# A fused attention and FFN block: seven products for eight in more of the first FFN product, with fills, row scales and loads rearranged

## The chip, the cores and the metric

The kernel runs on one core of one Trainium2 chip. The metric is the device time of one execution in microseconds (us). A kernel is run several times, and medians are quoted. The profile is that of one execution. It gives a *span*, the time from the core's first to its last recorded work. The listed time is a little longer than the span, by 1.2 to 1.6 us here, and that difference matters below.

Names used: PE is TensorE, PEld its weight load, DVE is VectorE, ACT is ScalarE, POOL is GpSimd, SP is SyncE. A *bank* is a PSUM bank of 512 fp32 columns. "K tile t" is the product that makes the keys of 128 tokens (10 PE instructions of 320 columns). A "chunk" is 512 tokens, and there are four of them.

## The reference

```python
def _layernorm(x, axis=-1, eps=1e-5):
    m = jnp.mean(x, axis=axis, keepdims=True)
    v = jnp.var(x, axis=axis, keepdims=True)
    return (x - m) / jnp.sqrt(v + eps)

# x (1, 2048, 640) bf16, wqkv (640, 1920), wo (640, 640), w1 (640, 1728), w2 (1728, 640)
def _A_ref(x, wqkv, wo):              # linear attention, 32 heads of 20
    qkv = (x @ wqkv).reshape(B, S, 3, H, Dh).transpose(2, 0, 3, 1, 4)
    q, k, v = qkv[0], qkv[1], qkv[2]
    phi = lambda t: jnp.where(t > 0, t + 1, jnp.exp(t)) + 1e-6
    pq, pk = phi(q), phi(k)
    kv = jnp.einsum("bhsd,bhse->bhde", pk, v)
    z = jnp.einsum("bhsd->bhd", pk)
    num = jnp.einsum("bhqd,bhde->bhqe", pq, kv)
    den = jnp.einsum("bhqd,bhd->bhq", pq, z)[..., None] + 1e-6
    return (num / den).transpose(0, 2, 1, 3).reshape(B, S, D) @ wo

def _B_ref(x, w1, w2):                # FFN: relu(x w1) w2
    return jnp.maximum(x @ w1, 0) @ w2

xn = _layernorm(x)
out = x + _A_ref(xn, wqkv, wo) * silu(_B_ref(xn, w1, w2))
```

## The kernel before

The first FFN product makes a transposed hidden layer `hT`: 13 blocks of 128 rows and a half block of 64, for each of the four chunks, each block five products of 512 columns along the contraction (640 = 5 x 128). Chunks 2 and 3 already go through a scheme of seven products for eight over 2 x 2 blocks: blocks i and i + 6, chunks 2 and 3, four of the five contraction tiles; the fifth is added as it is. Chunks 0 and 1 are done block by block, with the other products woven in:

```python
def H_mm(j, f, b=None):                     # a block of the first FFN product, conventionally
    b = nextb() if b is None else b
    src, keys = hsrc(j)
    sc.group("PE", [(lambda eng, k=k: eng.matmul(ps[b], lhsT=w1_col(k, P * f, P), rhs=src[:, k, :],
                                                 start=(k == 0), stop=(k == C - 1))) for k in range(C)], ...)
    return lambda: sc.op("ACT", ...activation(out=hT[:, f, schunk(j)], in_=ps[b], func=ACTF.Relu)...)
# ...
kat = [{5: 4, 7: 5, 9: 6, 11: 7}, {2: 8, 5: 9, 8: 10, 11: 11, 14: 12, 16: 13, 18: 14, 20: 15}]
lnat = [{9: 8, 11: 9}, {0: 10, 2: 11, 5: 12, 8: 13, 11: 14, 13: 15}]
for j in range(2):
    for n, item in enumerate(plans[j]):
        # ... Q_block or H_block
        if j == 1 and n == 0:
            scale_bcast()
            build_consts()                  # GpSimd's fills and masks
        if j == 1 and n >= 7 and n < 20:
            scale_h(n - 7)                  # chunk 0 of hT times its row scales, on VectorE
        # ...
        if n in kat[j]:                     # one K tile after every second or third block
            t = kat[j][n]
            K_mm(t, 0)
            K_exp(t, 0)
            K_relu(t, 0)
            K_fin(t)
```

The tokens of chunk 0 go into the first products centred but not yet divided by their deviation, so that PE can start early; the first blocks of `hT` are scaled afterwards. The scales come from a diagonal matrix that GpSimd makes and one product with ones:

```python
def scale_rows():
    sc.op("POOL", ... tensor_tensor(out=dg..., in0=ident..., in1=rsy[:, 0:4]..., op=ALU.mult) ...)
def scale_bcast():
    b = nextb()
    sc.group("PE", [lambda eng: eng.matmul(ps[b], lhsT=one, rhs=dg, start=True, stop=True)], ...)
```

A unit of the scheme (`h_unit`), its sums on VectorE and copies on ScalarE, with PE's products marked `mm`:

```python
def s1():  mm(1, ba, True); cp(ps[bb], ("ps", bb), ba)      # ScalarE writes one bank from another
def s5_(): mm(5, bc, True); cp(s5, skey, bc, ...)
def s6():  mm(6, ba);       tt(ps[bc], ps[ba], s5, ALU.add, ...)   # VectorE, in PSUM
def s2():  mm(2, bb);       relu("ACT", i, 2, bb)
def s7():  mm(7, ba);       cp(ps[bd], ("ps", bd), ba)
def s3():  mm(3, bc);       relu("ACT", i, 3, bc)
def s4():
    mm(8, ba)
    tt(dst, ps[ba], s5, ALU.add, ...)                        # VectorE, PSUM to SBUF
    # ... a max on VectorE
    mm(4, bd); relu("DVE", i + 6, 2, bd)
```

The place later in the kernel that the change touches too: `u_T(4)` is a sum of 2240 columns on VectorE that is wanted late, `kvs()` makes the masked copies of kv that the products with wo (`W_block`) want at once.

```python
divide(0)
load_recip(1)
load_recip(2)
u_T(4)
# ...
        if p == 0:
            if n == 0:
                kvs()
            if n == 1:
                W_block(0, 4)
```

## Time and profile before

| | before |
|---|---|
| time, median of 3 | 209.35 us (209.14 to 209.63) |
| profiled span | 209.0 us |
| listed time less span, all its runs in this study | 1.21 to 1.31 us |
| spans of its 34 timed runs beside the experiments | 207.6 to 209.5 us, median 208.2 |
| first 512-column product to first wo product, profiled run | 12.66 to 133.03 = 120.37 us |

The last row is *the stretch*. It starts with the first conventional FFN product, behind the head in which PE waits for data to land, and ends with the first product with wo. All of the change but its head lies inside.

How to read the views: in the chain of waits and the timeline the first two numbers are start and duration in us, then engine, tile and line. On the PE, pieces of the chain that abut are work back to back. L650 is the conventional FFN block, L1029 a product of the seven-for-eight scheme, L551 a K tile, L601 a Q block, L819 a sum or product of two tensors on VectorE, L1277 a wo product.

Three cautions. In the chain a piece that follows other work begins where that work ends, some 0.17 us after its own first instruction; a piece that follows a wait begins with its own first instruction. So 120.37 is 0.16 too short: by the first instructions in the timeline, 12.50 and 133.03 us, the stretch of before is 120.53. For the same reason the idle time in square brackets is some 0.16 us less than what the wait costs. And where a record of a product is missing (x29 for x30), the chain shows 0.05 us of "issue" that is no wait.

One thing beside the lines that the prediction shows: the timeline of GpSimd and VectorE where the masks are built.

```profile
35.34 1.80 POOL L433 MEMSET regH<- 128x2048 bf16 x1
35.43 1.94 DVE L489 TENSOR_SCALAR reg<-reg,mv,rsy 128x640 bf16<-128x640 bf16 x1 [0.99 <-POOL rsy L469]
```

This norm on VectorE ends at 37.37 us, 0.23 us after GpSimd's fill. Elsewhere a norm takes 0.39 to 0.45 us, but for one of 1.15 us at 19.33, beside GpSimd's 1.03 us for the diagonal matrix (19.27). The change moves the fill and drops the matrix.

### The profile page before, as it was taken

What the parts mean: (1) busy time and instruction counts of PE and PEld (TensorE: products, weight loads), DVE (VectorE), ACT (ScalarE), POOL (GpSimd) and SP (SyncE); (2) the same over time, 40 slices, a digit from 0 to 9 for tenths busy, and PEclk for the clock granted to TensorE, in tenths of its full rate; (3) what the DMA queues carried; (4) which work ended last, traced back from release to release, by engine and by line L of the source; (5) the groups of instructions that cost most, each with busy time, mean ns of one, the idle gap of its engine ahead of it and who ended that gap; (6) DMA issues with size and microseconds to landing.
All of it is one profiled execution on the core that took longest, in us unless ns stands there. A gap on an engine that the chain in (4) does not pass through costs nothing.

```text
span 209.0 us, 3733 instructions
## 1 busy us (share of the span) xinstructions
PE 205.1 (98%) x1401; PEld 127.0 (61%) x1401; DVE 165.0 (79%) x365; ACT 120.8 (58%) x243; POOL 21.3 (10%) x54
## 2 busy tenths in 40 slices
PE   8999999999999999999999999999999999999995
PEld 7755555545555444444456777677777777777773
DVE  3888757768999858686879759898888989897465
ACT  6497767787787987786563435362435254343531
POOL 1176015711210000000000000000000000000001
DMA  6998896130136000301224999246941010110103
GB/s 196 330 297 168 219 257 94 31 63 2 39 59 186 0 5 0 125 0 26 102 63 108 245 343 376 98 123 219 362 148 63 3 63 28 38 63 0 63 3 127
DMA packets 33063, 24.74 MB, mean 118 GB/s; under 512 B 12821, under 2 KB 33045, under 8 KB 33045
## 3 DMA queue, kind: packets, MB, share of 16 engines
q1 hardware_dynamic: 31813, 23.13, 39.2%
q10 hardware_dynamic: 1232, 1.37, 1.9%
q8 instruction: 11, 0.18, 0.4%
q14 instruction: 7, 0.06, 0.1%
HBM read 15.81 MB, written 5.24 MB: 101 GB/s over the span
## 4 chain that ended last, share of the span: by engine, by line
PE 86%; DVE 6%; DMA 5%; issue 1%; SPq 0%
PE psT L874 33%; PE psT L650 14%; PE psT L1029 11%; PE psT L551 11%; PE psT L601 10%; DMA reg<-in_B_w_dram 4%; DVE reg L819 2%; PE psT L1486 2%; DMA reg<-in_A_x_dram 1%; PE psT L668 1%; PE psT L1277 1%; DVE reg L1474 1%; DVE regE L819 1%; PE psT L525 1%; DVE pqT L812 1%
## 5 line engine op out<-in xcount | busy, mean ns | idle before, releaser
L874 PE MATMUL psT<-reg,regH 128*128 128x320 bf16 (+1 forms) x224 | 34.3, 299 | 0.0
L874 PE MATMUL psT<-reg 128*128 128x320 bf16 (+1 forms) x164 | 27.7, 299 | 0.0
L874 PEld LDWEIGHTS psT<-reg,regH 128*128 128x128 bf16 (+1 forms) x224 | 21.9, 98 | 8.5
L819 DVE TENSOR_TENSOR psT<-psT,reg 128x320 f32<-128x320 f32 (+1 forms) x33 | 16.4, 513 | 12.0 <-PE psT L874 8.8
L1311 ACT ACTIVATE wv_sb<-psT 128x320 bf16<-128x320 f32 x28 | 11.3, 436 | 25.2 <-PE psT L874 15.6
L601 PE MATMUL psT<-reg 128*128 128x512 bf16 x100 | 24.7, 379 | 0.0
L561 ACT ACTIVATE regE<-psT 128x640 bf16<-128x640 f32 x24 | 15.6, 701 | 8.1 <-PE psT L551 8.1
L874 PEld LDWEIGHTS psT<-reg 128*128 128x128 f16 (+1 forms) x164 | 16.0, 98 | 6.9 <-DVE regH L819 0.2
L881 ACT ACTIVATE psT<-psT 128x320 f32<-128x320 f32 x32 | 13.6, 426 | 11.2 <-PE psT L874 10.7
L881 ACT ACTIVATE reg<-psT 128x320 f32<-128x320 f32 (+1 forms) x24 | 10.4, 435 | 15.6 <-PE psT L874 13.6
L650 PE MATMUL psT<-reg 128*128 128x512 bf16 x75 | 18.5, 379 | 0.0
L654 ACT ACTIVATE regH<-psT 128x512 bf16<-128x512 f32 x28 | 16.5, 608 | 3.2 <-PE psT L650 3.2
L551 PE MATMUL psT<-reg 128*128 128x320 bf16 x120 | 18.3, 299 | 0.0
L461 DVE BATCH_NORM_STATS2 stats<-reg 128x6 f32<-128x320 bf16 x32 | 14.1, 475 | 4.7 <-DMA reg<-in_A_x_dram 4.7
L601 PEld LDWEIGHTS psT<-reg 128*128 128x128 bf16 x100 | 9.6, 98 | 11.0 <-issue 0.7
L551 PEld LDWEIGHTS psT<-reg 128*128 128x128 bf16 x120 | 11.7, 98 | 6.5
L1479 POOL TENSOR_TENSOR reg<-reg 128x224 bf16<-128x224 bf16 x1 | 0.6, 604 | 146.6 <-DVE reg L1474 146.6
L819 DVE TENSOR_TENSOR reg<-reg 128x1024 f16<-128x1024 bf16 (+6 forms) x17 | 13.6, 809 | 2.3 <-DMA reg<-in_B_w_dram 2.0
L650 PE MATMUL psT<-regX,reg 128*128 128x512 bf16 x65 | 14.8, 379 | 0.0
L874 PE MATMUL psT<-reg,pqT 128*128 128x320 bf16 (+1 forms) x72 | 14.7, 299 | 0.0
L1474 DVE TENSOR_TENSOR reg<-psT,wv_sb 128x640 bf16<-128x640 f32 (+2 forms) x16 | 11.7, 739 | 3.4 <-PE psT L874 1.8
L1029 PE MATMUL psT<-reg 128*128 128x512 bf16 x48 | 14.0, 379 | 0.0
(145 smaller groups left out, 354.1 us busy)
## 6 DMA issues: line engine op xcount, KB each, us to landing
reg<-in_B_w_dram SPq DMA_DIRECT2D x12, 320.0 KB, 6.0
scr<-rden SPq DMA_DIRECT2D x4, 640.0 KB, 8.8
reg<-in_A_x_dram SPq DMA_DIRECT2D x4, 640.0 KB, 6.5
out_dram<-reg SPq DMA_DIRECT2D x15, 160.0 KB, 1.9
reg<-in_A_x_dram SPq DMA_DIRECT2D x13, 160.0 KB, 5.0
regE<-scr SPq DMA_DIRECT2D x3, 640.0 KB, 8.1
reg<-in_A_wo_dram SPq DMA_DIRECT2D x6, 160.0 KB, 3.1
reg<-in_A_wqkv_dram SPq DMA_DIRECT2D x1, 800.0 KB, 5.3
```

What stands on the lines that cost most here:

```text
L461: sc.op("DVE", lambda eng: eng.bn_stats(stats[:, t, a, :], xv[:, HN * a:HN * (a + 1)]), R=[("xin", t % XR)], W=[("stats", t, a)])
L551: fns.append(lambda eng, a=a, k=k, lhs=lhs: eng.matmul(ps[b + a][:, 0:HN], lhsT=lhs, rhs=wk[:, k, HN * a:HN * (a + 1)], start=(k == 0), st ...
L561: sc.op("ACT", lambda eng: eng.activation(out=o_.rearrange("p (a n) -> p a n", a=2), in_=ps2(b, HN), func=func, scale=scale), R=[("ps", b) ...
L601: sc.group("PE", [(lambda eng, k=k: eng.matmul(ps[b], lhsT=wq[:, k, P * f:P * (f + 1)], rhs=xnT[:, j, k, :], start=(k == 0), stop=(k == C ...
L650: sc.group("PE", [(lambda eng, k=k: eng.matmul(ps[b], lhsT=w1_col(k, P * f, P), rhs=src[:, k, :], start=(k == 0), stop=(k == C - 1))) for ...
L654: return lambda: sc.op("ACT", lambda eng: eng.activation(out=hT[:, f, schunk(j)], in_=ps[b], func=ACTF.Relu), R=[("ps", b)], W=[("hT", j, f)])
L819: sc.op("DVE", lambda eng: eng.tensor_tensor(out=out, in0=in0, in1=in1, op=op), R=R, W=W, extra=extra)
L874: sc.group("PE", [(lambda eng, k=k, lhs=lhs, rhs=rhs: eng.matmul(ps[b][:, 0:HN], lhsT=lhs, rhs=rhs, start=(start and k == 0), stop=(k == n ...
L881: sc.op("ACT", lambda eng: eng.activation(out=dst, in_=ps[b][:, 0:HN], func=ACTF.Copy), R=[("ps", b)], W=[dkey], extra=extra)
L1029: sc.group("PE", [(lambda eng, k=k, lhs=lhs, rhs=rhs: eng.matmul(ps[b], lhsT=lhs, rhs=rhs, start=(start and k == 0), stop=(k == n - 1), sk ...
L1311: sc.op("ACT", lambda eng: eng.activation(out=g[:, HN * n:HN * (n + 1)], in_=ps[b][:, 0:HN], func=ACTF.Silu), R=[("ps", b)], W=[("g", sl, ...
L1474: sc.op("DVE", lambda eng: eng.tensor_tensor(out=tmpo[:, os_, lo:hi].rearrange(shp, a=na), in0=src, in1=g_of(t)[0][:, lo:hi].rearrange(shp ...
```

## The change

Intent: use the seven-for-eight scheme for chunks 0 and 1 too, in four of its six block pairs (blocks 0 to 3 with 6 to 9). Five blocks (4, 5, 10, 11, 12) stay conventional and come first, while x is still being normalised and transposed. K tiles 4 to 7 are made in a row between the two chunks of these blocks; one K tile goes into each unit. To make room on VectorE and GpSimd, the fill and the masks move to the idle head, the row scales come from four small products, and most of the scalings fall away, since the four units take normalised tokens. Weight pieces 2 and 5 are loaded first, being wanted first. `u_T(4)` moves behind the kv copies.

The diff, cut to its core:

```diff
     sc.op("DVE", lambda eng: eng.memset(zero[:, :], 0.0), W=[("zero",)])
+    sc.op("DVE", lambda eng: eng.memset(hT[:, NF, :], 0.0), W=[("hz",)])
 ...
-    w1_load(0, 2, "SP")
+    w1_load(2, 3, "SP")
+    w1_load(5, 6, "SP")
     x_load(4)
     x_load(5)
-    w1_load(2, 3, "SP")
+    w1_load(6, NW, "SP")
     x_load(6)
     x_load(7)
-    w1_load(3, NW, "SP")
+    for d in (0, 3):
+        w1_load(d, d + 1, "SP")
 ...
     def build_consts():
-        sc.op("POOL", lambda eng: eng.memset(hT[:, NF, :], 0.0), W=[("hz",)])
 ...
+    build_consts()
 ...
+        if whole:
+            fns.append(lambda eng: eng.matmul(ps[b][:, HN:512], lhsT=one, rhs=wk[:, 0, 0:512 - HN], start=False, stop=True,
+                                              skip_group_check=True))
 ...
-        sc.group("PE", [lambda eng: eng.matmul(ps[b], lhsT=one, rhs=dg, start=True, stop=True)], R=[("dg",)],
-                 W=[("ps", b)])
+        sc.group("PE", [(lambda eng, t=t: eng.matmul(
+            ps[b][:, P * t:P * (t + 1)], lhsT=rsyH[:, t:t + 1].to_broadcast([P, P]), rhs=ident[:, :],
+            start=True, stop=True)) for t in range(4)], R=[("rsyH",), ("ident",)], W=[("ps", b)])
 ...
-    kat = [{5: 4, 7: 5, 9: 6, 11: 7}, {2: 8, 5: 9, 8: 10, 11: 11, 14: 12, 16: 13, 18: 14, 20: 15}]
 ...
+    HP = (4, 5, 10, 11, 12)
 ...
+    for n, f in enumerate(HP):
+        H_block(0, f)
+        run(after[n])
+        if n == 3:
+            x_load(8, 2)
+            w_load(wq[:, :, :], A_wqkv[:, 0:D], ("wq",))
+    scale_rows()
 ...
+    for n in range(4):
+        K_tile(4 + n, 2 * (n % 2))
+        run(after[n])
+    x_load(10, 2)
 ...
+        if n == 1:
+            x_load(12, 2)
+            x_load(14, 2)
+            for d in (1, 4):
+                w1_load(d, d + 1, "SP")
 ...
+    units = [h_unit(i, 0) for i in range(4)]
 ...
+    units[0]["s1"]()
+    for i, u in enumerate(units):
+        ob = 4 * (i % 2)
+        t = 8 + i
+        u["s5"]()
+        K_mm(t, ob + 2, whole=True)
+        K_exp(t, ob + 2)
+        u["s6"]()
+        K_relu(t, ob + 2)
 ...
+    build_mv6()
 ...
-    u_T(4)
 ...
                 if n == 0:
                     kvs()
+                    u_T(4)
```

The variable `whole` adds a product over the 192 columns of a bank that the K tile leaves unwritten, because the next unit lets ScalarE write that bank and then adds products to it.

## The prediction

> **What bounds the kernel now.** I read three views in this order: the busy digits of the page (which engine has no gap), the chain of waits in order of time (is that engine's work really what the end follows back to), and the timeline where the change puts work.
>
> ```profile
> PE 205.1 (98%) x1401; PEld 127.0 (61%) x1401; DVE 165.0 (79%) x365; ACT 120.8 (58%) x243; POOL 21.3 (10%) x54
> ...
> PE   8999999999999999999999999999999999999995
> ```
>
> A full digit for PE is no proof, since ends of matmuls are modelled. The chain decides: its pieces abut, and their length is instruction count times a fixed pitch.
>
> ```profile
> 9.68 2.99 PE psT L551 x22
> 12.66 6.47 PE psT L650 x30
> 19.14 1.36 PE psT L551 x10
> 20.50 2.16 PE psT L650 x10
> 22.66 1.36 PE psT L551 x10
> ...
> 131.29 1.69 DVE reg L819 x2
> 132.98 0.05 issue
> 133.03 0.87 PE psT L1277 x4
> ```
>
> Read: 30 products of 512 columns in 6.47 us are 215.7 ns each, 10 of 320 columns in 1.36 us are 136 ns each, and each piece begins where the last ended. From 9.68 to about 114 us nothing but PE is on the chain, so there a product removed is worth its pitch, and nothing else is worth anything unless it makes PE wait. The last three lines show the one wait of PE behind another engine in the middle of the kernel. Its timeline:
>
> ```profile
> 130.07 1.60 PE L1251 MATMUL psT<-reg,wv_sb 128*128 128x120 bf16 x30
> ...
> 131.21 1.32 DVE L819 TENSOR_TENSOR reg<-reg,regX 128x2240 f16<-128x2240 bf16 x1
> ...
> 132.44 0.95 DVE L819 TENSOR_TENSOR reg<-psT,mv 128x360 bf16<-128x360 f32 x3
> ...
> 133.03 0.87 PE L1277 MATMUL psT<-reg 128*128 128x320 bf16 x4 [0.41 <-DVE reg L819]
> ```
>
> VectorE does a 2240-wide sum (u_T(4), needed only at the end of that unit) before the masked copies of kv that PE waits for; PE loses 0.41 us.
>
> **What the Trainium skill says.** (1) "TensorE: Matmul & The Clock Gate", section "Wait — 56ns, not 53.3ns?": warm back-to-back products start every N / 2.4 GHz + about 2.5 ns, 215.7 ns at N = 512. The trace agrees (215.7), and five 128-column transposes in 0.28 us agree with its 55.6. (2) "VectorE: DVE Perf Modes", section "Zero memsets can be issued as uint32 (trn2)": a memset takes a cycle per element whatever its type, and zeros may be issued as 4-byte words. At the page's 0.96 GHz I estimate 2.1 us for the 2048-wide fill, 1.1 us if issued as words; the trace has none of that size on VectorE. (3) "SBUF — State Buffer", section "Who interferes with whom": VectorE in a two-port mode and GpSimd block each other for a whole instruction. The trace agrees: the normalising step normally takes about 0.45 us and took 1.94 us at 35.43 beside GpSimd's 1.80 us fill at 35.34. (4) "PSUM — Partial Sum Buffer", section "The four PSUM rules": a first product clears the written bits of its whole bank, and ScalarE's writes don't set them. That is why the change adds a product over the other 192 columns after some K products; the trace of before has no such case.
>
> **The change part by part.**
>
> 1. Chunks 0 and 1 of the first FFN product. Before: 13 blocks x 2 chunks x 5 = 130 products of 512 columns. After: five blocks (4, 5, 10, 11, 12) as before, 5 x 2 x 5 = 50, and four units of 7 x 2 + 4 = 18 each, 72, in place of 80. Removed: 8 x 0.2157 = 1.73 us of PE. This is small because the five tiles along the contraction leave one that isn't shared out: 18 for 20, not 7 for 8. The half block is still 20 small products.
> 2. Added on PE: four 192-column products. Estimate from the skill's formula 192 / 2.4 + 2.5 = 82 ns, 0.33 us together. The row-scale broadcast goes from one 512-column product (0.22 us in the chain) to four of 128 (4 x 0.056 = 0.22 us): nothing.
> 3. u_T(4) moves after the kv products. VectorE reaches the masked copies at 131.2 instead of 132.44 us; three take 0.95 us, the first product of kv ended about 130.9, so they are done before PE has finished the seven products that start at 131.51 and end at 132.62. The 0.41 us wait should vanish.
> 4. VectorE: removed nine of 14 scalings at about 0.41 us (3.7 us). Added four 1024-wide sums of x, 4 x 0.69 = 2.7 us, and per unit one PSUM sum (0.70), one PSUM-to-SBUF sum (0.69) and a max (0.295), 4 x 1.68 = 6.7 us. Net +5.8 us, less some 2 us of collisions with GpSimd. From 9.68 to 70 us VectorE was busy 49.4 of 60.3 us; it becomes about 53 of 59, some 90%. ScalarE: four units of six evictions, 24, for 16 relus, +8 x 0.6 = 4.8 us on 47.4. Neither becomes the sum-bound engine.
> 5. The fill on VectorE runs between 0.92 us, when its first memset ends, and 3.36 us, when x lands: 2.44 us, room even for the 2.1 us form. GpSimd's masks (about 1.5 us by their rows at 37 to 39 us) fit behind the identity, which ends at 1.51 us. Hidden: nothing gained, nothing lost at the head. PE isn't helped, as x lands when it did.
> 6. Load order: the same x and wk come first; weight pieces 2 and 5 (320 KB each) replace 0 and 1. They land about 6 us after issue, near 10 us, and are wanted at 12.7 and 14.8 us: no wait.
>
> Sum on the path: -1.73 + 0.33 - 0.41 = -1.81 us, so 207.5 us if no new wait appears.
>
> **Rivals.**
>
> (a) Transposes too late for the early K tiles. Tiles 4 to 7 are now consumed after five blocks, in a row, instead of one per two blocks.
>
> ```profile
> 14.20 0.45 DVE L489 TENSOR_SCALAR reg<-reg,mv,rsy 128x640 bf16<-128x640 bf16 x1 [0.36 <-POOL rsy L469]
> ...
> 14.68 1.33 SPq L541 DMA_TRANSPOSE reg<-reg  x1
> ...
> 18.98 1.52 PE L551 MATMUL psT<-reg 128*128 128x320 bf16 x10
> ```
>
> The transfer queue's waits give 2.8 to 3.3 us from issue to landing here. PE reaches tile 4 at 12.66 + 25 x 0.2157 = 18.05 us, and the transposition lands at 14.68 + 3.3 = 17.98. With the sums of earlier tiles moved behind the norms I work out norms ending at about 16.0, 17.6 and 18.9 us and landings at 18.9, 20.4 and 21.8 us, wanted at 19.4, 20.8 and 22.1. It fits with 0.1 to 0.5 us to spare; a slip would cost 0.3 to 1.5 us. For: GpSimd's power step takes 0.57 to 0.83 us and each norm waits for it. Against: three of before's loads of x between these transposes are gone.
>
> (b) VectorE or ScalarE sets the pace in the four units. One unit is 18 x 0.2157 + 10 x 0.136 + 0.08 + 5 x 0.2157 = 6.4 us of PE. VectorE's worst is the second: 1.7 for the unit's own sums, four weight sums 1.7, a K tile's two steps 0.8, a Q block's two 0.7, one norm 0.45, one set of statistics 1.1: 6.4 us by row durations, about 5.6 by the spacing of back-to-back rows, since their ends overlap. ScalarE has eight 512-wide evictions and two 640-wide ones, about 5.3 us. Tight but under. PE tolerates about 0.8 us of VectorE's lag: between the product whose sum VectorE must read and the next product in that bank lie 3 + 5 products, 1.73 us, and the sum takes 0.70. If VectorE fell behind by a microsecond per unit, it would cost 2 to 4 us and the time would be 209.5 to 211.5.
>
> (c) Transposes of chunk 0 late. They now follow the 800 KB load of wq; beside such a load before they took 5.1, 4.6 and 3.7 us. I have them landing between 26 and 29 us, and PE wants them at 23.5 + 25 x 0.2157 + 0.22 = 29.1 us for the half block. Possible cost 0 to 1.5 us, which would then also delay VectorE's sums of x.
>
> (d) The 0.41 us only moves: the transfer of w2 (8.50 us in the chain, issued when PE frees w1) could set that stretch. It is triggered by PE, so it shifts along, and PE isn't kept waiting by it now. I give it one chance in four.
>
> **How the range follows.** PE's own account gives 207.5. I add 0.3 us for small waits of kinds (a) to (c), spread between 0 and 1.5: 207.8 us. The low end, 206.9, needs everything hidden and some small wait of before lost as well; 209.3 has 1.8 us of new waits, which eats the whole gain. Faster by over 2% means below 205.2, 2.3 us more than all products and waits removed add up to: 0.01. Slower by over 2% means above 213.5, six microseconds of new stalls, only if (b) goes badly wrong in all units: 0.03. Within 2%: 0.96.
>
> **What would show it.** Right: in the chain, 50 conventional first-FFN products between 12.7 and about 30 us in place of 130 up to about 70; 180 products of the seven-for-eight kind in place of 108; PE's pieces still abutting at 215.7 ns; the stage before the later units, which ended at 71.5 us, ending near 70.1; no wait of the 320-column wo products for a VectorE sum near 131 us; VectorE at 9's through the units while PE has no gap; no 1.9 us norm. Wrong: PE rows of K tiles with idle time released by a transposition at 18 to 23 us; idle PE in the units released by a VectorE sum on PSUM or by a ScalarE copy; the half block waiting near 29 us; or PE waiting at the head because VectorE's fill reaches past 3.4 us. If PE's contiguous stretch doesn't shorten by about 1.4 us, step 1 or 2 is wrong; if it does and the end moves less, a wait further on has taken it back.

## The result

| | before | after |
|---|---|---|
| time, median of 4 | 209.40 us (209.14 to 209.63) | 208.51 us (207.95 to 208.57) |
| after / before | | 0.9952 [0.9931, 0.9973] |
| profiled span | 209.0 us | 207.0 us |
| listed time less span | 1.21 to 1.31 us | 1.49 to 1.57 us |
| the stretch | 120.37 us | 12.58 to 131.41 = 118.83 us |
| VectorE busy, 9.7 to 70.2 us before, 9.6 to 69.0 us after | 49.6 of 60.5 us | 51.9 of 59.4 us |

A ratio here is the record's, with its 95% interval in brackets; it is worked out from the fast runs of the same rounds, so it is not quite the ratio of the medians. The change gives 0.5%, within 2%.

The page of the kernel after, first the busy times and instruction counts:

```profile
PE 203.6 (98%) x1400; PEld 126.3 (61%) x1400; DVE 169.7 (82%) x373; ACT 124.3 (60%) x251; POOL 18.0 (9%) x53
```

PE has one instruction fewer: eight products of 512 columns less, four of 192 columns more, three more for the scales. VectorE has eight more, ScalarE eight more. PE has lost 1.5 us of busy time, the others have gained or lost a few.

The chain of waits of the kernel after (L658 conventional FFN block, L556 K tile, L943 the row scales, L562 the 192-column product, L1320 wo):

```profile
12.58 5.40 PE psT L658 x25
17.97 2.72 PE psT L556 x20
20.69 0.03 issue
20.72 2.89 PE psT L556 x20
...
25.77 0.22 PE psT L943 x4
...
33.55 1.42 PE psT L556 x10
34.97 0.08 PE psT L562
...
131.41 0.54 PE psT L1320 x4
```

The pitch is unchanged: 25 products in 5.40 us are 216 ns each. K tiles 4 to 7, however, have lost something. The first two take 2.72 us, 136 ns a product, as before; the next two take 0.03 + 2.89 = 2.92. And the K tile of the first unit takes 1.42 where 10 x 136 ns is 1.36. The scales take 0.22 us and a 192-column product 0.08, as estimated. The wo products follow PE and nobody else.

The timeline of the kernel after, at the three places that changed:

```profile
1.12 0.91 DVE L401 MEMSET regH<- 128x1024 uint32 x1 [0.18 <-issue]
3.30 0.49 DVE L469 BATCH_NORM_STATS2 stats<-reg 128x6 f32<-128x320 bf16 x1 [1.27 <-DMA reg<-in_A_x_dram]
...
20.72 1.20 PEld L556 LDWEIGHTS psT<-reg 128*128 128x128 bf16 x10 [0.36 <-ACT regE L569]
22.07 1.20 PEld L556 LDWEIGHTS psT<-reg 128*128 128x128 bf16 x10 [0.16 <-ACT regE L569]
...
129.84 1.16 DVE L827 TENSOR_TENSOR reg<-psT,mv 128x360 bf16<-128x360 f32 x3 [0.57 <-PE psT L1294]
130.92 1.31 DVE L827 TENSOR_TENSOR reg<-reg,regX 128x2240 f16<-128x2240 bf16 x1
131.24 0.71 PE L1320 MATMUL psT<-reg 128*128 128x320 bf16 x4
```

First pair: the fill runs in VectorE's idle head and ends at 2.03 us; the first statistics still wait for x, at 3.30 us. Second pair: the weight loads of K tiles 6 and 7 are held up 0.36 and 0.16 us by L569, ScalarE's reading of the banks that tiles 4 and 5 used. Only two bank pairs serve four tiles in a row. Last three: the masked copies now come before the 2240-wide sum, and the wo products don't wait.

So the stretch went down by 1.54 us between these two profiles (1.70 by first instructions). The prediction's sum of steps was 1.81. The time went down by 0.9. The experiments had to say which parts of this are real in other executions, and where the rest stayed.

### The profile page after: what moved, and what is told of

Its sections match the earlier page's. It is cut to its first block, busy times and chain, and to the rows that moved or that the text cites. A ratio compares the mean times of both kernels' runs of the same rounds, so it can differ in the third digit from the quotient of the medians.

```text
span 207.0 us, 3745 instructions
## 1 busy us (share of the span) xinstructions
PE 203.6 (98%) x1400; PEld 126.3 (61%) x1400; DVE 169.7 (82%) x373; ACT 124.3 (60%) x251; POOL 18.0 (9%) x53
## 4 chain that ended last, share of the span: by engine, by line
PE 97%; DMA 1%; DVE 1%; issue 0%
PE psT L882 40%; PE psT L1036 19%; PE psT L556 11%; PE psT L609 11%; PE psT L658 6%; PE psT L1529 3%; PE psT L1580 2%; DMA reg<-in_A_x_dram 1%; PE psT L676 1%; PE psT L1320 1%; PE psT L530 1%; PE psT L1294 1%; PE psT L756 1%; PE psT L786 1%; PE psT L432 0%; DVE stats L469 0%
## 5 line engine op out<-in xcount | busy, mean ns | idle before, releaser
L609 PE MATMUL psT<-reg 128*128 128x512 bf16 x100 | 24.4, 379 | 0.0
L1036 PE MATMUL psT<-reg 128*128 128x512 bf16 x80 | 23.2, 379 | 0.0
L827 DVE TENSOR_TENSOR psT<-psT,reg 128x320 f32<-128x320 f32 x30 | 14.3, 493 | 9.3 <-PE psT L882 9.2
L889 ACT ACTIVATE reg<-psT 128x320 f32<-128x320 f32 (+1 forms) x24 | 10.4, 435 | 15.6 <-PE psT L882 13.6
L556 PE MATMUL psT<-reg 128*128 128x320 bf16 x120 | 17.9, 299 | 0.0
L1042 ACT ACTIVATE psT<-psT 128x512 f32<-128x512 f32 x20 | 11.9, 595 | 8.2 <-PE psT L1036 8.2
L569 ACT ACTIVATE regE<-psT 128x640 bf16<-128x640 f32 x24 | 15.6, 706 | 1.9 <-PE psT L556 1.2
L609 PEld LDWEIGHTS psT<-reg 128*128 128x128 bf16 x100 | 9.6, 98 | 11.6 <-issue 0.7
L1048 ACT ACTIVATE regH<-psT 128x512 bf16<-128x512 f32 (+1 forms) x24 | 14.5, 604 | 2.1 <-PE psT L1036 1.8
L556 PEld LDWEIGHTS psT<-reg 128*128 128x128 bf16 x120 | 11.5, 98 | 6.5 <-ACT regE L569 0.5
L827 DVE TENSOR_TENSOR reg<-reg 128x1024 f16<-128x1024 bf16 (+6 forms) x17 | 13.5, 805 | 1.7 <-DMA reg<-in_B_w_dram 1.2
L1036 PEld LDWEIGHTS psT<-reg 128*128 128x128 bf16 x80 | 7.7, 98 | 9.4 <-issue 0.4
```

The lines of the kernel that those rows point to most:

```text
L556: fns.append(lambda eng, a=a, k=k, lhs=lhs: eng.matmul(ps[b + a][:, 0:HN], lhsT=lhs, rhs=wk[:, k, HN * a:HN * (a + 1)], start=(k == 0), st ...
L569: sc.op("ACT", lambda eng: eng.activation(out=o_.rearrange("p (a n) -> p a n", a=2), in_=ps2(b, HN), func=func, scale=scale), R=[("ps", b) ...
L609: sc.group("PE", [(lambda eng, k=k: eng.matmul(ps[b], lhsT=wq[:, k, P * f:P * (f + 1)], rhs=xnT[:, j, k, :], start=(k == 0), stop=(k == C ...
L827: sc.op("DVE", lambda eng: eng.tensor_tensor(out=out, in0=in0, in1=in1, op=op), R=R, W=W, extra=extra)
L889: sc.op("ACT", lambda eng: eng.activation(out=dst, in_=ps[b][:, 0:HN], func=ACTF.Copy), R=[("ps", b)], W=[dkey], extra=extra)
L1036: sc.group("PE", [(lambda eng, k=k, lhs=lhs, rhs=rhs: eng.matmul(ps[b], lhsT=lhs, rhs=rhs, start=(start and k == 0), stop=(k == n - 1), sk ...
```

## The experiments

Theory: PE bounds the kernel; the gain is the eight products less the four small ones, less some waits for banks around the K tiles, and the late sum adds little. Rivals: the late sum is worth its 0.4 us and something at the head takes it back; or VectorE paces the four units and eats part of the eight products; or transpositions that land late do. There were twelve runs in three groups; each group shares its runs of the kernel before, with medians of 209.41, 209.20 and 209.48 us.

| run | median us | ratio to before | listed less span | the stretch |
|---|---|---|---|---|
| e1, before, sum late | 209.22 | 1.0000 [0.9960, 1.0039] | 1.22 to 1.33 | 119.95 |
| e2, after, sum early | 208.49 | 0.9954 [0.9919, 0.9989] | 1.49 to 1.57 | 118.77 |
| e3, after, 8 products more | 210.01 | 1.0025 [0.9996, 1.0054] | 1.50 to 1.57 | 120.50 |
| e4, after, third bank pair | 208.58 | 0.9951 [0.9918, 0.9985] | 1.47 to 1.55 | about 118.9 |
| e5, before, fills at the head | 209.69 | 1.0017 [0.9994, 1.0040] | 1.49 to 1.56 | 119.95 |
| e6, after, three mends | 209.14 | 0.9990 [0.9961, 1.0019] | 1.46 to 1.56 | 119.19 |
| e7, after, 8 maxes more a unit | 215.05 | 1.0265 [1.0232, 1.0299] | 1.51 to 1.56 | about 126.6 |
| e8, after, old load order | 209.73 | 1.0019 [0.9995, 1.0043] | 1.47 to 1.58 | 118.72, from 13.84 |
| e9, after, fill on GpSimd at the head | 208.59 | 0.9950 [0.9927, 0.9972] | 1.22 to 1.32 | about 120.4 |
| e10, after, masks late | 208.46 | 0.9948 [0.9926, 0.9970] | 1.48 to 1.56 | 118.77 |
| e11, after, third bank pair and later loads | 208.31 | 0.9937 [0.9915, 0.9959] | 1.51 to 1.60 | 118.57 |
| e12, after, four mends | 208.73 | 0.9960 [0.9941, 0.9980] | 1.24 to 1.33 | about 119.3 |

All twelve gave right results. Five are single parts of the change done or undone (e1, e2, e5, e8, e9), two add cost (e3, e7), e10 parts the masks from the fill, and the others try to get lost tenths back. Where the chain doesn't hold both ends of the stretch ("about", and e8), it is taken from the first instructions in the timeline.

### e1: the late sum alone, in the kernel before

```diff
     load_recip(2)
-    u_T(4)
 ...
                 if n == 0:
                     kvs()
+                    u_T(4)
```

> The kernel before with one thing from the change: the 2240-wide sum u_T(4) is issued after the kv products instead of ahead of them. Theory A (the profile of before holds in every run: PE waits 0.41 us and then 0.33 us more for the masked copies, which the two profiles show as 0.74 us gone): 0.5 to 0.8 us faster than before, ratio 0.996 to 0.9975. Theory B (in most timed runs of before the late landing of w2 that pushes VectorE into this wait is earlier, and the wait is small): within 0.2 us of before, ratio 0.999 to 1.001, and the spans listed for the runs of before are near 208, not 209.0.

Measured: 209.22 us against 209.41, ratio 1.0000. Its chain of waits:

```profile
12.35 6.47 PE psT L650 x30
...
132.30 0.54 PE psT L1277 x4
```

The wait is gone from this profile, and the stretch is 119.95 us, 0.42 less than in the profiled run of before (0.58 by first instructions). Yet the time did not move, as theory B had it, and the spans of before have a median of 208.2 us: the profiled 209.0 was one of its slower executions. The interval reaches 0.4% to either side, so 0.4 us is not excluded by time alone; e5 says more below.

### e2: the change without the late sum

```diff
+    u_T(4)
 ...
                     kvs()
-                    u_T(4)
```

> The changed kernel with u_T(4) put back ahead of the kv products. Theory A: 0.5 to 0.8 us slower than the changed kernel, so about 209.1 us or ratio 0.998 to 0.999 to before. Theory B: no slower than the changed kernel by more than 0.2 us, ratio 0.995 to 0.9965.

Measured: 208.49 us, ratio 0.9954, where the full change has 0.9952. In its chain the first four wo products begin at 131.15 us, a stretch of 118.77, and take 0.73 us instead of 0.54: a wait of 0.19 us for the last of the masked copies. The order of the sum is worth 0.2 us at most in this execution.

### e3: eight products put back

```diff
+            first = [lambda eng: eng.matmul(ps[b], lhsT=l_[0][0], rhs=l_[0][1], start=True, stop=False, skip_group_check=True)]
-            sc.group("PE", [(lambda eng, k=k, lhs=lhs, rhs=rhs: eng.matmul(
+            sc.group("PE", (first if start and jp == 0 else []) + [(lambda eng, k=k, lhs=lhs, rhs=rhs: eng.matmul(
```

Two products a unit are done twice, the second time over the first, so the result stays right and PE has the eight products back, with nothing else changed.

> The changed kernel with eight 512-wide products put back: in each of the four new units the first product of two groups is issued twice, so that PE does 20 per unit as without the seven-for-eight form; all results stay right. Theory PE-bound (nothing but the number of products counts in the units): 8 x 0.216 = 1.73 us slower than the changed kernel, about 210.2 us, ratio 1.003 to 1.0045, with VectorE and ScalarE the same. Rival (VectorE or ScalarE sets the pace of the units): less than 1 us slower than the changed kernel.

Measured: 210.01 us, 1.5 over e2 and 1.5 over the change. The chain:

```profile
12.26 5.40 PE psT L658 x25
...
132.76 0.54 PE psT L1321 x4
```

The stretch is 120.50, 1.67 us over the 118.83 of the change and 1.73 over the 118.77 of e2 and e10, against 8 x 0.2157 = 1.73. So in these units a PE product costs its whole pitch. If VectorE or ScalarE had set the pace, the added products would have been partly free.

### e4: a third pair of banks for the K tiles

```diff
-        K_tile(4 + n, 2 * (n % 2))
+        K_tile(4 + n, (0, 2, 6, 0)[n])
```

> The changed kernel with the K tiles 4 to 7 in bank pairs 0, 2, 6, 0 instead of 0, 2, 0, 2. In the trace of after PE waits there for ScalarE to empty the pair (weight loads held 0.36 and 0.16 us, the 40 products take 5.64 us instead of 5.43). Theory: the wait is for the banks, so the 40 products take 5.43 us and the kernel gains 0.2 us, ratio to before 0.9935 to 0.995. Rival (the wait is for the transposition of tile 6, put down to the other): no change, and the wait stays.

Measured: 208.58 us, ratio 0.9951. PE's timeline:

```profile
17.28 5.60 PE L556 MATMUL psT<-reg 128*128 128x320 bf16 x40
...
33.00 1.52 PE L556 MATMUL psT<-reg 128*128 128x320 bf16 x10 [0.18 <-DMA reg<-reg]
```

The forty products now run without a break: the next product starts at 22.72 us, 5.44 after the first of them, where the change took 5.64 with its 0.03 of issue. So the 0.20 us there is a wait for banks. The gain did not reach the end: the K tile of the first unit now waits for its transposition, which had been issued at 27.39 us and landed 5.48 us later. The row has 0.18 us idle; the product starts 0.34 later than at the pitch. PE had got there earlier than the data: it had left the head at 12.06 us, 0.5 before the profiled run of the change. This is the first of several places where the schedule has no slack left.

### e5: the fills at the head, in the kernel before

```diff
+    sc.op("DVE", lambda eng: eng.memset(hT[:, NF, :], 0.0), W=[("hz",)])
 ...
     def build_consts():
-        sc.op("POOL", lambda eng: eng.memset(hT[:, NF, :], 0.0), W=[("hz",)])
 ...
+    build_consts()
 ...
                 scale_bcast()
-                build_consts()
```

> The kernel before with only the fills moved: the 2048-wide zero fill on VectorE at the head and GpSimd's masks in the idle head. Theory (nothing of it is on the path): same time as before, ratio 0.999 to 1.001; no normalising step near 1.9 us any more. Second question: the listed time is 1.3 us above the span in every run of before and of e1, but 1.5 us in the runs of the changed kernel and of e2 to e4. If the fills make that 0.2 us, this kernel shows 1.5; if the other load order or the sevens do, it shows 1.3.

Measured: 209.69 us against 209.20, ratio 1.0017. The listed time exceeds the span by 1.49 to 1.56 us, where the kernel before has 1.21 to 1.31 in all its runs. That is 0.25 us lost outside of what the profile records, with the same products and loads inside. The time alone says less: 1.0017 is above the expected 0.999 to 1.001, but the interval includes 1. The chain:

```profile
12.45 0.05 issue
...
132.40 0.59 PE psT L1276 x4
```

The stretch is 119.95, just as in e1, although here the sum is still early: 0.05 us of wait is left in the wo products. VectorE reached the sum 0.46 us after PE began the kv products (130.31 and 129.85 us in the timeline); in the profiled run of before it was 1.14 us (131.21 and 130.07). So the wait that the prediction priced at 0.41 us comes in some executions and hardly in others; I take 119.95 for the undisturbed stretch of before.

What sets it is the landing of a piece of w2. VectorE waits for it, and works without a gap from there to the 2240-wide sum. First before, then e5:

```profile
123.11 1.33 DVE L819 TENSOR_TENSOR reg<-reg 128x2240 f16<-128x2240 bf16 x1 [1.99 <-DMA reg<-in_B_w_dram]
...
122.21 1.32 DVE L819 TENSOR_TENSOR reg<-reg 128x2240 f16<-128x2240 bf16 x1 [1.30 <-DMA reg<-in_B_w_dram]
```

From this row to the late sum are 8.10 us in both, and in e2 too (121.10 to 129.20). But the row comes 6.96 us ahead of PE's first kv product in before, 7.64 in e5 and 7.50 in e2, and the wait falls with it: 0.41 and 0.33 us, 0.05, 0.19.

### e6: three mends at once

```diff
-        K_tile(4 + n, 2 * (n % 2))
+        K_tile(4 + n, (0, 2, 6, 0)[n])
 ...
-        if n == 1:
+        if n == 3:
             x_load(12, 2)
             x_load(14, 2)
             # ... weight pieces 1 and 4
 ...
-        K_mm(t, ob + 2, whole=True)
-        K_exp(t, ob + 2)
+        K_mm(t, ob + 1, halves=(1, 0), st=2)
+        K_exp(t, ob + 1, 2)
```

The third pair of banks, the later loads (so that they don't share the transfer engines with the transposition of tile 8), and the unit's K tile in two banks that the next unit starts afresh, so that no 192-column product is needed.

> A version meant to beat both: the changed kernel with (1) K tiles 4 to 7 in bank pairs 0, 2, 6, 0, (2) the K tiles of the units in banks that need no 192-column product (the two banks whose next group starts afresh), (3) the loads of x 12 to 15 and of weight pieces 1 and 4 issued after the transposition of tile 9 instead of before it, so that tile 8 lands in about 3 us instead of 5.2 to 5.5. Theory (PE sets the pace and these are the waits): the stretch from the first 512-column product to the first wo product falls from 118.83 us by 0.2 + 0.33 + 0.06 to about 118.25 us; time about 207.9 us, ratio to before 0.991 to 0.993. Rival (the wait of e4 comes from VectorE's and GpSimd's chain to tile 8, not from the loads): tile 8 still waits about 0.2 us and the stretch is 118.4 to 118.6.

Measured: 209.14 us, ratio 0.9990: by the medians 0.6 us slower than the change, though the intervals of the ratios overlap, and 0.36 us in the stretch. Groups of waits (waiting tile and line, what it waited for: us in total, times, longest):

```profile
PE psT L556 <- ACT pqT L619: 0.3, 1, 0.3
...
PE psT L556 <- DVE regH L824: 0.3, 1, 0.3
```

The saved 0.33 us are the four small products; in their place PE waits for ScalarE and VectorE, which still read the other two banks, and the weight loads wait a further 1.2 us in three instances. The small product is the cheaper choice. The third mend did not do what was expected of it either: with the loads issued later, the transposition of tile 8 still landed 5.0 us after its issue, not 3.

### e7: VectorE loaded

```diff
+            if jp == 0:
+                for _ in range(8):
+                    sc.op("DVE", lambda eng: eng.tensor_scalar(out=dst, in0=dst, scalar1=0.0, scalar2=None, op0=ALU.max),
+                          R=[("hT", j1, i + 6)], W=[("hT", j1, i + 6)])
```

> The changed kernel with the max at the end of each of the four units repeated eight times on VectorE (same result), some 8 x 0.25 = 2 us more of VectorE per unit of 6.4 us. In the trace of after VectorE is busy about 5.4 of 6.4 us in a unit. Theory (VectorE has about 1 us of room per unit): two microseconds more overfill it by about 1 us per unit, so 3 to 4.5 us slower than the changed kernel, about 212 us, and PE gets gaps in the units. Rival (VectorE lags harmlessly and catches up in the K tiles behind): under 1 us slower.

Measured: 215.05 us, 6.5 over the change. This was more than expected, because the eight maxes, each dependent on the one before, filled not 2 but 2.59 us: 10.4 us in all. Of these 10.4 us, 3.9 were hidden by the medians, about 1 us a unit. That is how much room VectorE has. The busy times say the same: in the four units of the change, from 36.1 to 61.0 us, VectorE was busy 21.4 of 24.9 us, so 0.9 us free a unit. Once the room is used up, PE waits for VectorE's sums in PSUM, as rival (b) had it:

```profile
PE psT L1036 <- DVE psT L827: 4.8, 3, 2.0
```

In the change itself no such wait exists. Together with e3 this takes rival (b) off the list.

The profile has another wait, ahead of the first unit, where the code is still that of the change:

```profile
30.01 1.26 PE L676 MATMUL psT<-reg 128*32 128x512 bf16 x20 [1.48 <-DMA reg<-reg]
```

The half block waits for the transpositions of chunk 0, the last of which was issued at 27.21 us, 1.1 later than in the change, and landed 2.71 later. So rival (c) does bite in some executions. The profiled run took 215.65 us, as one other did; the remaining two took 214.11 and 214.46. Without the 1.65 us that the product starts late here, its stretch is 6.1 us over the change's and 4.2 were hidden, again about 1 us a unit.

### e8: the old load order

```diff
-    w1_load(2, 3, "SP")
-    w1_load(5, 6, "SP")
+    w1_load(0, 1, "SP")
+    w1_load(3, 4, "SP")
 ...
-    for d in (0, 3):
+    for d in (2, 5):
```

> The changed kernel with weight pieces 0 and 3 loaded first and 2 and 5 last. The first conventional blocks use pieces 2, 2, 5, 5, 6. Theory: pieces 2 and 5 are issued some 4 to 5 us later and land near 15 to 17 us; PE wants piece 2 at 12.6 us, so it waits 2 to 4 us in the head and the kernel is 1.5 to 4 us slower than the changed kernel. Rival (the load order is only tidying): no change.

Measured: 209.73 us, 1.2 over the change, less than I had expected at the least. PE's timeline:

```profile
13.84 5.51 PE L658 MATMUL psT<-regX,reg 128*128 128x512 bf16 x24 [1.96 <-ACT regE L569]
```

The first blocks wait 1.96 us. The row names ScalarE, but its row of eight evictions (L569) runs on past this point in the change too, where the first weight load comes 2.1 us after that row begins; here it comes 4.1 us after. The piece of weights that these blocks read was issued at 8.26 us and landed 5.2 us later, at 13.5, just before that weight load (13.59). The time is only 1.2 us longer (1.4 when each kernel is set against its own runs of before), and nothing was made up further on: from 13.84 us the stretch is 118.72. PE had left the head about 0.7 us earlier in this execution than in the profiled run of the change, so that its first product came 1.43 us later than there (12.41), not 2. The load order is a needed part of the change that only prevents a loss: it gains nothing over the kernel before.

### e9: the fill on GpSimd, still at the head

```diff
-    sc.op("DVE", lambda eng: eng.memset(hT[:, NF, :], 0.0), W=[("hz",)])
 ...
     def build_consts():
+        sc.op("POOL", lambda eng: eng.memset(hT[:, NF, :], 0.0), W=[("hz",)])
```

> The changed kernel with the 2048-wide zero fill on GpSimd again, but at the head, ahead of the masks. e5 showed that moving the fills alone adds about 0.25 us between the span and the listed time (1.53 against 1.27 us). If VectorE's fill makes it, the difference falls back to about 1.3 us here and the time to about 208.25 us; if the masks at the head make it, it stays at 1.5 us.

Measured: 208.59 us, ratio 0.9950. Listed time less span is back at 1.22 to 1.32 us. With e5 this pins the 0.25 us on VectorE's fill: every kernel of this study that has it shows 1.46 to 1.60, every one without it 1.21 to 1.33. The time did not drop with it, though, since spans of its runs were 206.6 to 208.0 us. Its profile shows why:

```profile
PE psT L556 <- ACT psT L1042: 0.8, 1, 0.8
...
PE psT L676 <- DMA reg<-reg: 0.6, 1, 0.6
```

The half block (L676) waited 0.6 us for the transpositions of chunk 0, which landed 6.6, 6.0, 5.3 and 3.0 us after their issue beside the load of wq, and the first unit's K tile 0.8 us for the transposition of tile 8 (the row names ScalarE; the transposition landed 6.2 us after 28.02, and PE started then). In the change the same transpositions took 5.6, 4.1, 3.5, 2.7 and 5.2 us and PE waited for none of them by more than 0.06. GpSimd's fill is not needed for this: e7 has the fill on VectorE and waits longer at the same place. And it is not only the transfers. The last transposition of chunk 0 landed at 29.1 us, 0.3 later than in the change (28.8), but PE was ready for the half block at 28.4, 0.7 earlier, since it had left the head earlier. This is the slowest of the six runs (209.26 us), so its 1.4 us of waits are not the typical case.

### e10: the masks late, the fill at the head

```diff
-    build_consts()
 ...
     x_load(10, 2)
+    build_consts()
```

> The changed kernel with the zero fill on VectorE at the head as it is, but GpSimd's masks built after the early K tiles, near 25 us, as before the change. If VectorE's fill makes the 0.25 us outside the span, the difference stays at 1.5 us; if the masks at the head make it, it falls to about 1.3 us. The span should stay within 0.3 us of 207.0, or rise by some tenths where GpSimd's masks hold up a reciprocal root of a norm.

Measured: 208.46 us, listed less span 1.48 to 1.56, the stretch 12.51 to 131.28 = 118.77. So it isn't GpSimd's masks in the head that lengthen the listed time, it is VectorE's fill; and PE's stretch is the same with the masks built early (e2) or late.

### e11: the third bank pair with later loads

```diff
-        K_tile(4 + n, 2 * (n % 2))
+        K_tile(4 + n, (0, 2, 6, 0)[n])
 ...
-        if n == 1:
+        if n == 3:
             x_load(12, 2)
             x_load(14, 2)
             # ... weight pieces 1 and 4
```

> The changed kernel with two of the three mends of e6: bank pairs 0, 2, 6, 0 for K tiles 4 to 7 and the loads of x 12 to 15 and of weight pieces 1 and 4 after the transposition of tile 9; the 192-column products stay, since e6 showed that the banks without them make PE wait for VectorE. Theory: tile 8 now lands some 2 us earlier than in e4, the wait of 0.18 us there goes, and the stretch from the first 512-column product to the first wo product falls from 118.83 to about 118.6 us; ratio to before about 0.994. Rival (the wait at tile 8 comes from the engines ahead of the transposition): stretch stays at 118.8 to 118.9.

Measured: 208.31 us, ratio 0.9937. The chain:

```profile
12.57 5.40 PE psT L658 x25
17.97 5.43 PE psT L556 x40
...
33.34 1.36 PE psT L556 x10
```

The K tiles take 5.43 us and that of the first unit 1.36. The first wo product starts at 131.14 us, the stretch is 118.57, 0.26 less than in the change, which is 0.20 + 0.06. The 0.20 is the third bank pair, as in e4 and e6. That the later loads are behind the 0.06 is not shown. The transposition of tile 8 landed 3.6 us after issue in place of 5.2, but it did so in e2 and e10 as well, which have the loads where the change has them, no such wait, and a stretch of 118.77, 0.20 over this one; in e6, with the later loads, it took 5.0. What the later loads do change is tile 9: 3.2, 4.0 and 2.6 us in e6, e11 and e12 against 4.7 to 7.7 in the change and the seven runs that load as it does. PE waits for tile 9 in none of them. This is the best version by median and mean. By time alone it can't be told from the change (intervals 0.9915 to 0.9959 and 0.9931 to 0.9973).

### e12: e11 with the fill on GpSimd and wq loaded at the head

```diff
     # e11 and e9, and:
     for d in (0, 3):
         w1_load(d, d + 1, "SP")
+    w_load(wq[:, :, :], A_wqkv[:, 0:D], ("wq",))
 ...
         if n == 3:
             x_load(8, 2)
-            w_load(wq[:, :, :], A_wqkv[:, 0:D], ("wq",))
```

> The last run, a version meant to beat both: the changed kernel with e11's two mends, e9's fill on GpSimd at the head, and the 800 KB load of wq issued right behind weight pieces 0 and 3 (about 10 us) instead of just ahead of the transpositions of tiles 0 to 3, which landed 5.6 to 6.6 us after issue beside it in after and e9 and made PE wait 0.6 us in e9. Theory (shared transfers are what makes the stretch vary): those transpositions land in about 3 us, no PE wait on a transposition, the stretch from the first 512-column product to the first wo product is 118.4 to 118.7 us, the listed time is 1.27 us above the span, and the time about 207.9 us, ratio 0.991 to 0.993. Rival: the earlier load delays the transpositions of tiles 4 to 7 instead, PE waits at the first K tile, and nothing is won.

Measured: 208.73 us, ratio 0.9960, spans 207.2 to 207.7. The 0.25 us outside the span is saved (1.24 to 1.33), but PE lost more than that inside, 0.74 by the stretch against e11:

```profile
18.24 5.61 PE L557 MATMUL psT<-reg 128*128 128x320 bf16 x40 [0.57 <-DMA reg<-reg]
```

The load of wq, moved out of the way of chunk 0's transpositions, now stands in the way of tile 4's, which landed 3.92 us after issue where it took 2.6 to 2.7 in the change. In both places tried, the 800 KB stand beside transpositions that PE wants with little slack.

## Why the prediction was right, and which of its terms were not

The prediction was 207.8 us with a range from 206.9 to 209.3 and 0.96 for "within 2%"; the time was 208.51. It was right, in the upper half of its range, and the sum behind it was 1.0 us too good. Term by term:

1. **Eight products removed, 1.73 us.** Right. e3 puts them back for 1.67 to 1.73 us on the chain and 1.5 us in time. PE does bound this part, and the count is what mattered: 18 for 20 in a unit, not 7 for 8.
2. **Four 192-column products, 0.33 us.** Right. The row has 0.08 us, so 0.32 together. The scales are 0.22 us in the chain before and after.
3. **The 0.41 us wait of the wo products.** The place was right and the wait is gone, but the term was mis-sized. It was read from one profile and counted as a gain of every run. In that profile it was even 0.74 us: after the 0.41 ahead of the first wo product, the four took 0.87 us and not 0.54. In e5, with the sum just as early, it was 0.05; in e2, 0.19. Doing the move alone (e1) or undoing it alone (e2) didn't move the time. The rival (d), "only moves", is not what happened: nothing else came in its place. But (d) had named the transfer that sets the size of the wait, the landing of w2 (e5). By the spans, most executions had little to remove.
4. **Work of VectorE and ScalarE.** Right. VectorE was busy 51.9 us where I had about 53, of 59.4; no norm of 1.9 us is left. Rival (b) didn't come, but its room was about 1 us a unit (e7), so the estimate of "tight but under" was a fair one. (The tolerance of "about 0.8 us" doesn't follow from its own figures, which give 1.73 - 0.70 = 1.03. ScalarE's 5.3 us a unit is less than its rows add up to, 8 x 0.6 + 2 x 0.7 = 6.2, but near the 5.1 that it was busy.)
5. **Fill and masks at the head, "nothing gained, nothing lost".** Half wrong. Inside the span this is so: the fill ended at 2.03 us, the masks at about 3.1, PE started as before. But the listed time is longer than the span by 0.25 us more with VectorE's fill there (e5, e9, e10). No step of the prediction looked at that difference. Its cause is open: it lies outside of what the profile records.
6. **Load order.** Right, and needed: with the old order PE waits 1.96 us at once and the time is 1.2 us longer (e8).

Of the small waits for which the prediction added 0.3 us, 0.26 came in the profiled run: 0.20 at K tiles 6 and 7 and 0.06 at tile 8 (e2 and e10 have only the 0.20). That the allowance had the right size was luck: rival (a) had named the place but not the cause. It feared late transpositions; those landed in 2.6 to 2.7 us, in time. The wait was for banks: two pairs for four tiles in a row (e4). Rival (c), the transpositions of chunk 0, did not bite in the profiled run of the change, but in e7, with the same code up to there, it did for 1.5 us, and in e9 for 0.6. So it can lengthen the change too; how often it does, a few runs of each kernel with one profile don't tell.

One sign that the prediction had set was wrong. It said that if PE's contiguous work doesn't shorten by about 1.4 us, step 1 or 2 is wrong. Up to the later units it shortened by 1.13 (12.66 to 71.49 before, 12.58 to 70.28 after), and yet both steps held: the sign had left out the waits for banks.

The ledger of the stretch: undisturbed before 119.95 (e1, e5), after 118.83, so -1.12 us. The terms: -1.73 + 0.33 + 0.20 + 0.06 = -1.14. With +0.25 outside the span this is -0.9; measured -0.89 by the medians. With an interval of 0.2% to either side, 0.4 us, that the two agree to a hundredth is luck; it is the terms seen in the traces that carry the account. The expected -1.81 fell short by 0.41 (the wait that is mostly not there), 0.26 (of which 0.3 had been allowed for) and 0.25 (outside the span).

What the runs leave open: why VectorE's fill in the head lengthens the listed time and not the span; why the transpositions of chunk 0 and of tile 8, and the piece of w2, land at such different times in executions of the same code; and whether a kernel with both e11's mends and a cheaper place for the fill gets the 0.25 us as well, since e12 changed the place of wq with it.

## What to carry to other kernels

Where one engine has no gap, price a change by counting that engine's instructions at their measured pitch; that part of the sum held to 0.06 us here. A wait that one profile shows may be in that execution only: look for it in a second profile before it is counted as a gain, and compare a stretch between two marks on the bounding engine rather than whole spans, which the head shifts by half a microsecond. Such a stretch is not free of the head either: where PE left it early, it came to data that had not landed (e4, e9). A tighter schedule uses up the slack of everything that feeds it (banks, transpositions beside large loads), so each tenth won back tends to uncover the next wait, and a mend is best tried alone before it is stacked on others.

## What the Trainium skill lacked or had wrong

- "VectorE: DVE Perf Modes", section "Zero memsets can be issued as uint32 (trn2)": the trace agrees. The fill of 128 x 2048 bf16 was issued as 1024 uint32 elements without being asked for, and took 0.91 us; a cycle an element at the page's 0.96 GHz would be 1.07 us, an estimate from that page which the row undercuts.
- That a fill on VectorE at the head lengthens the listed time but not the span is on none of the pages that I read: 1.46 to 1.60 us lie between the two with it, 1.21 to 1.33 without (e5 adds it to the kernel before, e9 takes it out of the kernel after).
- "DMA: Bandwidth & Descriptors", section "Latency and other measured facts", gives a bandwidth for transpositions (261 GB/s in one kernel). It doesn't say how far one is delayed beside plain loads: in the change a 128 x 640 bf16 transposition landed 2.6 to 2.7 us after its issue at 14.6 to 18.9 us, 5.6 beside the 800 KB load of wq, and 6.3 (tile 9) right behind loads of x and weights; with those loads issued later, tile 9's took 2.6 to 4.0. The same transposition of tile 8 took 2.8 to 6.2 us from run to run.
- The other places cited held: 215.7 ns a product of 512 columns and 0.08 us one of 192 columns for "TensorE: Matmul & The Clock Gate", and for "SBUF — State Buffer" the norm of 1.94 us beside GpSimd's fill, gone when the fill was moved. What is cited of "PSUM — Partial Sum Buffer" no run here tests: all kernels that need the 192-column product have it.
